# Fused threshold attention and bilinear ffn: v made stationary, x produced transposed, ffn per batch, and TensorE held to the written order

## The chip, the cores and the metric

The kernel runs on one core of a Trainium2 chip. The metric is device time in microseconds (us). Executions of one kernel on one chip agree within about 1%; times are medians of several runs. All runs compared below are of the fast state unless it is said otherwise.

The engines are TensorE (PE; its weight loads are listed as PEld), VectorE (DVE), ScalarE (ACT), GpSimd (POOL) and the DMA queues that SyncE (SP) starts. They run side by side and wait for one another by semaphores.

## The reference, cut to what matters

```python
# q, k, v: (8 batches, 8 heads, 576 positions, 64), float32
scores = q @ k.transpose(0, 1, 3, 2) / 8
thresh = max(scores, axis=-1) - tau
scores = where(scores >= thresh, scores, -1e9)
attn   = softmax(scores)                        # (denominator + 1e-9)
x      = (attn @ v) as (4608 tokens, 512)       # heads side by side
out    = ((x @ w_a) * (x @ w_b)) @ w_out        # 512 -> 1536 -> 512
```

The three weight matrices arrive as float64. The kernel turns their bits into float32 on the chip, in 36 pieces of 128 x 512. All products are of float32.

## The kernel before

Two heads of a batch are a pair. A pair is five units of query rows: four main units (128 rows of each head) and a tail unit (the last 64 rows of both heads). There are 32 pairs and 160 units. A unit goes through `scores`, `weigh` (exponent, mask, row sums), `turn` (transposes of the weights on TensorE) and `weighted` (weights times v). The ffn of two batches is spread between the units of the next two. In `weighted` the weights are stationary and v is streamed:

```python
def weighted(i, u):                       # before, cut
    pv = ps_1.tile([P, 2, D], ...)
    for j in range(2):                    # head
        for c in range(NCB + 1):          # block of keys
            ...                           # lhsT (stationary): 128 keys x 128 queries; rhs: 64 columns of v
            nc.tensor.matmul(dst, lhsT, rhs, start=(c == 0), stop=(c == NCB))
    ...                                   # then scaled by 1/sum, and transposed by finish()
```

One piece of weights is converted with five VectorE operations, one of ScalarE and three of GpSimd. The first one of GpSimd is a clamp:

```python
nc.gpsimd.tensor_scalar(top, top, float_of(0x47F00000), float_of(0x38000000),
                        op0=ALU.min, op1=ALU.max)
...
nc.gpsimd.tensor_tensor(low, low, t, op=ALU.mult)
nc.gpsimd.tensor_tensor(low, low, top, op=ALU.add)
```

## Time and profile before

| | before |
|---|---|
| time, median of 3 first runs | 2063.77 us |
| TensorE busy | 97% of the span |
| first ffn matmul | 363 us, after 40 units of attention alone |
| VectorE / ScalarE / GpSimd busy | 36% / 28% / 14% |

Two more views: the first is the chain that ended last, the path of work and waits followed back from the end, as shares of the span by engine:

```profile
PE 89%; POOL 3%; DVE 3%; ACT 2%; issue 1%; SPq 1%; DMA 0%; POOLq 0%; DVEq 0%; ACTq 0%
```

The second is the list of groups of GpSimd. The columns are line, engine, operation, tiles, shapes and count, then busy us and mean ns of one, then the idle time before them and what ended it:

```profile
L150 POOL TENSOR_TENSOR low<-low,top 128x512 f32<-128x512 f32 x36 | 46.3, 1287 | 2.3
L149 POOL TENSOR_TENSOR low<-low,t 128x512 f32<-128x512 f32 x36 | 46.0, 1277 | 39.3 <-DVE t L148 20.4 <-ACT wT L270 15.1 <-ACT low L140 3.4
L142 POOL TENSOR_SCALAR top<-top 128x512 f32<-128x512 f32 x36 | 22.1, 613 | 36.4 <-DVE sums L251 35.6 <-DVE top L141 0.8
```

### The profile page before, as it was taken

The page shows a single profiled execution, that of the slowest core. Times are in us where ns is not written, and L with a number is a line of the kernel's source. Part 1 is how long each engine was busy: PE and PEld are TensorE (multiplying, and loading weights), DVE is VectorE, ACT ScalarE, POOL GpSimd, SP SyncE. Part 2 cuts the span into 40 slices and gives each one's busy share as a digit, 9 for nine tenths or more (in the row PEclk, how much of TensorE's full clock was granted, in tenths as well). Part 3 has the DMA queues.
Part 4 walks back from the last instruction along what each step waited for, and adds up shares of the span by engine and source line. Part 5 has one row for each costly group of instructions (what it writes and reads, how often), then busy time and mean ns, then how long its engine had stood idle before and what let it go on. Part 6 is the DMA issues. An engine that isn't in the chain of part 4 may idle for free.

```text
span 2066.4 us, 24299 instructions
## 1 busy us (share of the span) xinstructions
PE 2002.3 (97%) x9472; PEld 1308.9 (63%) x9472; DVE 753.0 (36%) x1866; ACT 571.1 (28%) x1017; POOL 297.0 (14%) x728
## 2 busy tenths in 40 slices
PE   7788888999999999999999999999999999999999
PEld 5577776665665666665665666666666666655554
DVE  6776765333332333333332332333333333200000
ACT  3444433222222232322222332332222322200000
POOL 4555552000000000000000000000000000000000
PEclk9767767999999999999999999999999999999999
DMA  4322321000001001001000000000100000000000
GB/s 124 86 79 72 90 76 28 18 18 22 17 18 28 17 18 33 18 7 28 23 18 22 23 18 17 23 19 23 28 12 23 16 1 6 11 6 10 11 5 16
DMA packets 125826, 58.20 MB, mean 28 GB/s; under 512 B 116496, under 2 KB 116496, under 8 KB 125712
## 3 DMA queue, kind: packets, MB, share of 16 engines
q1 hardware_dynamic: 120528, 47.21, 9.1%
q10 hardware_dynamic: 5184, 9.44, 1.2%
q8 instruction: 75, 1.23, 0.2%
q14 instruction: 39, 0.32, 0.0%
HBM read 47.19 MB, written 9.44 MB: 27 GB/s over the span
## 4 chain that ended last, share of the span: by engine, by line
PE 89%; POOL 3%; DVE 3%; ACT 2%; issue 1%; SPq 1%; DMA 0%; POOLq 0%; DVEq 0%; ACTq 0%
PE pab L328 36%; PE po L344 18%; PE pv L287 15%; PE sc L222 9%; PE tp L265 6%; PE sc L225 2%; PE tp L269 1%; ACT w L244 1%; POOL low L150 1%; POOL low L149 1%; DVE mx L232 1%; POOL bias L233 1%; ACT wT L266 1%; PE tp L309 1%; DVE w L247 1%
## 5 line engine op out<-in xcount | busy, mean ns | idle before, releaser
L328 PE MATMUL pab<-xT,wa_sb 128*128 128x384 f32 x1152 | 409.3, 490 | 2.2 <-ACT wT L266 2.0
L328 PE MATMUL pab<-xT,wb_sb 128*128 128x384 f32 x1152 | 408.9, 489 | 0.0
L344 PE MATMUL po<-wo_sb,h 128*128 128x512 f32 x864 | 389.7, 596 | 0.1
L232 DVE TENSOR_REDUCE mx<-sc 128x1 f32<-128x576 f32 x288 | 208.1, 753 | 414.4 <-PE sc L222 350.1
L287 PEld LDWEIGHTS pv<-vm,wT 128*128 128x128 f32 (+1 forms) x2560 | 310.3, 193 | 61.8 <-issue 25.4
L287 PE MATMUL pv<-vm,wT 128*128 128x64 f32 (+1 forms) x2560 | 323.2, 276 | 9.9 <-ACT wT L266 9.2
L266 ACT COPY wT<-tp 128x512 f32<-128x512 f32 x288 | 159.1, 589 | 553.2 <-PE tp L265 552.9
L328 PEld LDWEIGHTS pab<-xT,wa_sb 128*128 128x128 f32 x1152 | 211.9, 190 | 133.3 <-ACT wT L266 4.4
L328 PEld LDWEIGHTS pab<-xT,wb_sb 128*128 128x128 f32 x1152 | 212.4, 190 | 130.2
L233 POOL TENSOR_SCALAR bias<-mx,e_nscale 128x1 f32<-128x1 f32 x288 | 99.3, 345 | 1331.0 <-DVE mx L232 1294.7
L244 ACT ACTIVATE w<-sc,bias,e_scale 128x576 f32<-128x576 f32 x288 | 233.2, 845 | 194.3 <-POOL bias L233 188.6
L247 DVE SCALAR_TENSOR_TENSOR w<-sc,thr,w 128x576 f32<-128x576 f32 x288 | 227.8, 815 | 138.9 <-ACT w L244 137.0
L344 PEld LDWEIGHTS po<-wo_sb,h 128*128 128x128 f32 x864 | 157.7, 191 | 163.9 <-issue 159.6
L222 PE MATMUL sc<-kT,qT 64*128 64x64 f32 (+1 forms) x1024 | 222.3, 486 | 37.3 <-DVE w L247 37.0
L222 PEld LDWEIGHTS sc<-kT,qT 64*128 64x128 f32 x1024 | 113.6, 203 | 169.1 <-issue 148.1
L338 DVE TENSOR_TENSOR h<-a,pab 128x384 f32<-128x384 f32 x144 | 79.7, 553 | 353.7 <-PE pab L328 353.7
L335 ACT COPY a<-pab 128x384 f32<-128x384 f32 x144 | 69.6, 484 | 473.0 <-PE pab L328 471.0
L265 PE MATMUL tp<-ident,w 128*128 128x128 f32 x1152 | 181.9, 304 | 0.8 <-DVE qT L202 0.7
L265 PEld LDWEIGHTS tp<-ident,w 128*128 128x128 f32 x1152 | 144.7, 157 | 18.7 <-DVE qT L202 5.0
L291 DVE TENSOR_TENSOR x<-pv,rcp 128x128 f32<-128x128 f32 x128 | 37.1, 290 | 243.2 <-PE pv L287 243.1
L287 PE MATMUL pv<-vt,wT 128*128 128x64 f32 (+1 forms) x640 | 123.4, 276 | 0.0
L287 PEld LDWEIGHTS pv<-vt,wT 128*128 128x128 f32 (+1 forms) x640 | 96.7, 193 | 8.1 <-ACT low L140 3.8
(57 smaller groups left out, 958.1 us busy)
## 6 DMA issues: line engine op xcount, KB each, us to landing
out_dram<-osb ACTq DMA_DIRECT2D x36, 256.0 KB, 2.0
qm<-in_q_dram SPq DMA_DIRECT2D x64, 128.0 KB, 2.9
km<-in_k_dram SPq DMA_DIRECT2D x64, 128.0 KB, 3.0
vm<-in_v_dram SPq DMA_DIRECT2D x64, 128.0 KB, 2.7
raw<-in_moe_w_a_dram SPq DMA_DIRECT2D x12, 512.0 KB, 3.5
raw<-in_moe_w_b_dram SPq DMA_DIRECT2D x12, 512.0 KB, 3.6
raw<-in_moe_w_out_dram SPq DMA_DIRECT2D x12, 512.0 KB, 3.5
qt<-in_q_dram SPq DMA_DIRECT2D x32, 32.0 KB, 2.4
```

The source lines that it names most:

```text
L222: nc.tensor.matmul(sc[j][:, c0:c1], qT[r, u * P:(u + 1) * P], kT[r, c0:c1], start=True, stop=True)
L232: nc.vector.tensor_reduce(mx[:, c], sc[j], axis=AX.X, op=ALU.max)
L233: nc.gpsimd.tensor_scalar(bias[:, c], mx[:, c], e_nscale[:, 0:1], None, op0=ALU.mult)
L244: nc.scalar.activation(w, s, AF.Exp, bias=bias[:, j:j + 1], scale=e_scale[:, 0:1])
L247: nc.vector.scalar_tensor_tensor(out=ws[j], in0=s, scalar=thr[:, j:j + 1], in1=ws[j], op0=ALU.is_ge, op1=ALU.mult, accum_out=sums[:, j:j + 1])
L265: nc.tensor.transpose(tp[:, c, :], w[:, c * P:(c + 1) * P], ident)
L266: nc.scalar.copy(wT[:, j, 0:NCB, :], tp)
L287: nc.tensor.matmul(dst, lhsT, rhs, start=(c == 0), stop=(c == NCB))
L328: nc.tensor.matmul(p, w[:, c, fs], xT[:, c, t0:t0 + NTB], start=(c == 0), stop=(c == HP - 1))
L335: nc.scalar.copy(a, p)
L338: nc.vector.tensor_tensor(h, a, pab[1], op=ALU.mult)
L344: nc.tensor.matmul(po, hs[F][:, u * P:(u + 1) * P], wo_sb[:, F, :], start=(F == 0), stop=(F == NF - 1))
```

## The change

The intent has four parts. v becomes the stationary operand, with 64 columns, so the two heads use the two column halves of TensorE's array of multipliers and x comes out transposed without further transposes. The ffn runs per batch in groups of 512 tokens, with all tails as a ninth group, so it can start after one batch. The weights are therefore divided by their row sums before they are transposed, on GpSimd. And TensorE keeps the order in which the instructions are written, while the other engines are still reordered by a scheduler. The conversion of a weight piece also loses one VectorE operation, and the two bounds of its clamp change places.

```diff
-        nc.gpsimd.tensor_scalar(top, top, float_of(0x47F00000), float_of(0x38000000),
-                                op0=ALU.min, op1=ALU.max)
+        nc.gpsimd.tensor_scalar(mag, mag, float_of(0x38000000), float_of(0x47F00000),
+                                op0=ALU.max, op1=ALU.min)
 ... (rest of the conversion cut: one VectorE operation less)
     def weigh(i, u):
 ...
         nc.vector.reciprocal(rcp[:, 0:n], sums[:, 0:n])
+        for j in range(n):
+            nc.gpsimd.tensor_scalar(ws[j], ws[j], rcp[:, j:j + 1], None, op0=ALU.mult)
 ...
     def weighted(i, u):
-        for j in range(2):
-            for c in range(NCB + 1):
-                rhs = vm[:, c, j, :] if c < NCB else vt[:, j, :]
+        for c in range(NCB + 1):
+            for j in range(2):
                 if u < NCB:
-                    dst, lhsT = pv[:, j, :], wT[:, j, c, :]
+                    rhs = wT[:, j, c, :] if c < NCB else wTt[:, 0, :]
 ...
-                nc.tensor.matmul(dst, lhsT, rhs, start=(c == 0), stop=(c == NCB))
+                nc.tensor.matmul(pv[j * D:(j + 1) * D, 0:cols],
+                                 vm[:, j, c, :] if c < NCB else vt[:, j, :],
+                                 rhs, start=(c == 0), stop=(c == NCB))
 ... (finish(), which transposed x, is gone; ffn(g) takes 512 tokens in place of 3 x 384)
+    ctx.enter_context(tc.manual_schedule(engines={mybir.EngineType.PE}))
-    per_group = GB * HP * (NCB + 1)
+    per_group = HP * (NCB + 1)
 ...
-        convert_weights()
-        load_weights(1)
+        for _ in range(n % 2 if n < per_group else 2):
+            convert_weights()
+            load_weights(1)
```

## The prediction

> **What bounds the kernel now.** I read the page top down: busy shares, slices, groups, then the timeline of one steady unit. Rows of the page:
>
> ```profile
> span 2066.4 us, 24299 instructions
> PE 2002.3 (97%) x9472; PEld 1308.9 (63%) x9472; DVE 753.0 (36%) x1866; ACT 571.1 (28%) x1017; POOL 297.0 (14%) x728
> ...
> PE   7788888999999999999999999999999999999999
> ...
> DVE  6776765333332333333332332333333333200000
> ...
> PEclk9767767999999999999999999999999999999999
> ```
>
> TensorE is the bound, in two stages. In the first seven slices (about 358 us) it runs at three quarters of its clock and not full, while VectorE has its highest load. These are the 40 units of query rows of the first two batches: attention alone, beside the conversion of the weights. After that TensorE is full at full clock. The table of stretches says it with numbers (columns: us, then busy us and instruction counts of PE, PEld, DVE, ACT, POOL, then clock, DMA share, GB/s):
>
> ```profile
> 12.00:358.00 346.00, 299.76 (x1550) 237.09 (x1550) 237.50 (x562) 139.92 (x234) 173.19 (x261) 0.75 0.29 79
> ...
> 400.00:1800.00 1400.00, 1393.90 (x6946) 899.96 (x6945) 477.03 (x1217) 394.25 (x715) 117.40 (x437) 1.00 0.07 19
> 1800.00:2064.00 264.00, 262.75 (x744) 141.13 (x742) 18.71 (x34) 21.04 (x42) 0.00 (x0) 1.00 0.02 8
> ```
>
> Busy time of matmuls overlaps, so I price them by the distance from the start of one row to the start of the next in the timeline of TensorE (start us, us, engine, line, operation, tiles, shapes, count):
>
> ```profile
> 1846.05 24.20 PE L344 MATMUL po<-wo_sb,h 128*128 128x512 f32 x56
> ...
> 1012.41 1.30 PE L222 MATMUL sc<-kT,qT 64*128 64x512 f32 x8
> 1013.64 0.66 PE L265 MATMUL tp<-ident,w 128*128 128x128 f32 x4
> 1014.13 0.27 PE L269 MATMUL tp<-ident,w 128*128 128x128 f32 x1
> 1014.24 0.49 PE L328 MATMUL pab<-xT,wb_sb 128*128 128x384 f32 x1
> ...
> 1042.07 1.00 PE L287 MATMUL pv<-vm,wT 128*128 128x64 f32 x8
> 1042.90 0.39 PE L287 MATMUL pv<-vt,wT 128*128 128x64 f32 x2
> 1043.13 1.06 PE L287 MATMUL pv<-vm,wT 128*128 128x64 f32 x8
> 1044.02 0.39 PE L287 MATMUL pv<-vt,wT 128*128 128x64 f32 x2
> 1044.24 1.51 PE L328 MATMUL pab<-xT,wa_sb 128*128 128x384 f32 x4
> ```
>
> Each fp32 matmul is two records ("passes"), a transpose is one. A 512-column pass costs (24.20 - 0.59)/55 = 0.429 us, the 384-column pass 0.3225 us (8 passes in 2.58 us in the last stage): the same per column. A score pair of two heads is 1.23 us, a transpose 0.12 us (five in 0.60), and the 20 passes of the weighted sum 1042.07 to 1044.24 = 2.17 us, 0.1085 each. That last pass streams 64 columns, which by the rate above would take 0.054 us: it is held up by the load of its 128-column weights.
>
> **What the Trainium skill says.** (1) "TensorE: Matmul & The Clock Gate", LDWEIGHTS: load time is the column count over 1.2, so 107 ns for 128 columns and 53 ns for 64, whatever the rows. The trace agrees: 0.1085 us with 128 columns, and 0.057 us in the tails, which load 64 (1.13 us for 20). (2) "TensorEngine Tiling (Array Packing)", When to Use Tiling, names this change: for a streamed dimension of 64, swap stationary and streaming and tile the columns, up to 2x. It also says under Key Properties that a change of mode drains the array. That two column halves overlap with fp32 here is shown by the tail units, where the second head follows the first in the other 64 columns:
>
> ```profile
> 1018.72 0.22 PE L287 MATMUL pv<-vt,wT 128*64 128x64 f32 x1
> 1018.77 0.22 PE L287 MATMUL pv<-vm,wT 128*64 128x64 f32 x1
> 1018.78 0.22 PE L287 MATMUL pv<-vt,wT 128*64 128x64 f32 x1
> 1018.83 0.46 PE L287 MATMUL pv<-vm,wT 128*64 128x64 f32 x5
> ```
>
> In program order both vt passes of head 0 come before the vm passes of head 1; here they alternate, two starting 10 ns apart, so the halves run side by side. Row halves do so too: a score pair holds four 512-column passes (4 x 0.429 = 1.72 us) and takes 1.23. (3) "SBUF — State Buffer", Who interferes with whom: VectorE and GpSimd exclude each other on a shared port. The trace shows it: one bitwise step of the conversion took 0.42 us alone and 1.35 us beside GpSimd's 1.27 us product. This matters for stage one.
>
> **The change part by part.**
>
> *ffn.* Before: 4 groups x 3 x 96 x 2 = 2304 passes of 384 and 864 of 512: 743 + 371 = 1114 us. After: nine groups (eight batches and one of all tails), 1728 + 864 passes of 512: 2592 x 0.429 = 1113 us. Nothing gained.
>
> *Attention on TensorE, per pair of heads.* Before: a main unit is 1.23 + 10 x 0.12 + 2.17 = 4.60 us; the tail unit 1.02 (scores) + 5 x 0.12 + 1.13 + 0.65 (four transposes of x and the fold) = 3.40; the preparation of q and k 1.28. A pair is 4 x 4.60 + 3.40 + 1.28 = 23.1 us.
> After: v is stationary with 64 columns, so loads (53 ns) hide under 128 streamed columns (107 ns), and the two heads alternate in the two column halves: ten matmuls x 2 passes at two abreast = 10 x 0.1085 = 1.09, with 0.1 for the drain 1.19 us. A main unit has nine transposes (both last 64-column blocks share one): 1.23 + 1.08 + 1.19 = 3.50. The tail: scores in two halves 1.02 again, six transposes 0.72, sum about 0.65, no transpose of x: 2.39. Preparation: nine transposes, 1.08. A pair is 17.5 us, 5.6 less.
>
> *Stage one.* It shrinks from 40 units to 20, as the ffn now starts after one batch. But the instruction order built from the changed kernel puts 31 of the 36 weight conversions into these 20 units (VectorE, ScalarE and GpSimd are still reordered; only TensorE is pinned). VectorE then has 31 x (0.730 + 0.629 + 0.680 + 0.417 = 2.46) = 76 us, one step of 0.69 less per piece than before, and attention: per main unit 2 x (0.753 + 0.815 + 0.083) + 0.33 = 3.63, per tail 1.95, preparation 1.56, so 18.0 per pair, 72 for four. Together 148 us. Before, VectorE was 69% busy there (237.5 of 346). TensorE's work falls from 185 us to 70 and no longer competes, and the exponent no longer waits for GpSimd's bias (188.6 us of ScalarE's waits before), so I choose 80%: 185 us, plus 12 until the first loads land, about 200 us. Before it was 358.
>
> *Stage two.* The scheme must reproduce the kernel before: 24 pairs x 23.1 + 1114 = 1668 us against 2066 - 358 = 1708 measured, so 40 us for 120 units, 0.33 us each, for drains and short waits. After: 28 pairs x 17.5 = 490, ffn 1113, 140 x 0.33 = 46.
>
> *The written order.* TensorE now waits where the text says. Units last about 10 us. The weights of a unit are masked about 6 us after its scores start, then scaled on GpSimd (two at about 0.69 us, scaled from the 0.613 us of a 512-column one): about 8 us, and the transposes come at 11. Score buffers come free at about 6 us and are wanted at 10. Those fit. One does not: in every fourth unit the preparation takes three of the four PSUM buffers just ahead of the transposes. VectorE copies q only after two reductions (2 x 0.753 + 0.682 = 2.2 us after the scores), TensorE wants that buffer 1.1 + 0.5 = 1.6 us after: with the semaphores some 0.8 us x 28 = 22 us.
>
> *Off the path.* Scaling of x on VectorE (37.1 + 18.1 us) goes, pv copies come to ScalarE, 288 scalings (some 200 us) to GpSimd at 14%. None becomes a bound in stage two: VectorE has about 4.5 us per 10 us unit.
>
> Sum: 200 + 490 + 1113 + 46 + 22 + 4 for the last output = **1875 us**, 9% less.
>
> **The rivals.**
> *The column halves run one after the other.* Then a weighted sum stays at 2.17 us (107 ns of streaming takes the place of 107 ns of loading), and the tail scores double: 112 x 0.98 + 28 x 1.36 = 148 us back, 2020 us. The alternation in the tail rows speaks against it.
> *The pinned order starves TensorE.* Before, the reordering left 0.5% idle after 400 us. If each of 140 units lost 1 us more, 2015 us. Against it: the slack of 2 to 4 us above.
> *Stage one becomes a conversion bound.* Twice as many pieces per unit, excluding each other on the shared port: at 60% VectorE it would take 260 us, 1935 in all; at 95% 170 and 1845.
>
> **Range and chances.** Stage one gives +50/-30 us, stalls +40/-30, the halves a one-sided +148 at some 6%. So 1820 to 1935 for 8 in 10. Faster by over 2%: 0.93; within 2%: 0.05 (halves serial, or starvation); slower: 0.02.
>
> **What would show it.** In the profile after: three or four slices of reduced clock in place of seven, the first ffn matmul near 200 us; from a pv row to the next row 1.2 us in place of 2.17, the two heads' records starting in pairs; 2592 ffn passes at 0.429; a wait of the transposes for the copy of q, about 28 times; PE near full from 220 us on. The number is wrong if the pv passes stand 0.107 us apart singly, if waits of TensorE for ScalarE or GpSimd add up to over 60 us in stage two, or if the ffn begins after 260 us.

## The result, and the profile after

The changed kernel takes 1974.33 us (median of 4 runs, 1973.8 to 1974.51) against 2065.66 us for the kernel before in the same session. The ratio is 0.956, 95% interval 0.9526 to 0.9594. A ratio here is the mean time of one kernel's fast runs over that of the other's of the same rounds, so it is not quite the ratio of the medians quoted. The direction was right and the size was not: 1875 us had been forecast, with 1935 as the upper end.

The page of the kernel after, its busy shares and some of its slices:

```profile
span 1972.5 us, 22785 instructions
...
PE 1801.7 (91%) x8704; PEld 951.7 (48%) x8704; DVE 703.9 (36%) x1598; ACT 554.2 (28%) x1141; POOL 722.6 (37%) x600
...
PE   4556569999999999999999999999999999999999
...
POOL 6888894233323333333323333333323332300000
PEclk9666679999999999999999999999999999999999
```

TensorE has less to do than before and idles more: its low stretch still fills six slices of 49 us, although it now covers 20 units instead of 40. What stands at 8 and 9 in those slices is GpSimd, whose busy time rose from 297 to 723 us.

The table of stretches (us, then busy us and counts of PE, PEld, DVE, ACT, POOL, then clock, DMA share, GB/s) puts the boundary at the first ffn matmul, which the timeline has at 259.8 us:

```profile
10.00:260.00 250.00, 140.55 (x773) 100.33 (x774) 149.66 (x295) 80.33 (x154) 211.93 (x149) 0.70 0.30 88
...
308.00:1600.00 1292.00, 1258.92 (x6586) 661.25 (x6585) 467.79 (x1130) 405.35 (x854) 427.84 (x376) 1.00 0.09 23
```

In stage one GpSimd is busy 212 of 250 us (85%), VectorE 150 (60%), TensorE 141 at 0.70 of its clock. In stage two TensorE is busy 97%. The chain of the kernel after, to be read against that of before:

```profile
PE 80%; POOL 9%; DVE 7%; issue 3%; ACT 1%; SPq 0%; DMA 0%; POOLq 0%; DVEq 0%
```

GpSimd went from 3% to 9% of the chain. Its two groups:

```profile
L258 POOL TENSOR_SCALAR w<-w,rcp 128x576 f32<-128x576 f32 x288 | 500.8, 1749 | 355.2 <-DVE rcp L256 333.1 <-PE pab L317 20.8 <-DVE mag L152 1.3
L146 POOL TENSOR_SCALAR mag<-mag 128x512 f32<-128x512 f32 x36 | 73.1, 2030 | 24.6 <-DVE mag L145 16.2 <-DVE rcp L256 6.4 <-DVE sums L255 2.0
```

A scaling takes 1.749 us, where 0.69 had been reckoned. The clamp, with the same two bounds on a tile of the same size, went from 0.613 to 2.030 us. TensorE's own waits, from the list of who waited for whom (us in total, times, longest):

```profile
PE tp L271 <- POOL w L258: 85.1, 47, 7.1
...
PE tp L271 <- DVE qT L199: 30.2, 27, 1.1
```

The transposes of the weights waited 85 us for GpSimd's scalings. The second wait is the one that the prediction named for the written order. The weighted sum did what was expected of it (timeline of TensorE, a main unit: start us, us, engine, line, operation, tiles, shapes, count):

```profile
1512.36 1.09 PE L294 MATMUL pv<-wT,vm 128*64 128x128 f32 x16
1513.29 0.39 PE L294 MATMUL pv<-wTt,v_tail 128*64 128x128 f32 x4
1513.60 1.30 PE L223 MATMUL sc<-kT,qT 64*128 64x512 f32 x8
```

From 1512.36 to 1513.60 is 1.24 us for twenty passes, in place of 2.17.

**Where the 97 us went.** The device time missed 1875 us by 99, the profile's span (1972.5 us) by 97; the table adds up to the span. From the starts of consecutive ffn groups in the timeline of TensorE, one can compare each part with the prediction's terms. The prediction's stage two comes to 203.4 us per batch that has both attention and ffn: (490 + 46 + 22)/7 = 79.7 us for its 20 units and 1113/9 = 123.7 us for its ffn.

| part of the kernel after | predicted us | measured us | difference |
|---|---|---|---|
| start to first ffn matmul (20 units) | 200 | 260 | +60 |
| first batch with ffn | 203.4 | 225.5 | +22 |
| six further batches | 1220.3 | 5 x 206.3 + 203.5 = 1235.0 | +15 |
| two last ffn groups and the output | 251 | 252 | +1 |

### The profile page after: what moved, and what is told of

Same layout as the page of the kernel before. It is cut to its first block, busy times and chain, and to the rows that moved or that the text cites. A ratio compares the mean times of both kernels' runs of the same rounds, so it can differ in the third digit from the quotient of the medians.

```text
span 1972.5 us, 22785 instructions
## 1 busy us (share of the span) xinstructions
PE 1801.7 (91%) x8704; PEld 951.7 (48%) x8704; DVE 703.9 (36%) x1598; ACT 554.2 (28%) x1141; POOL 722.6 (37%) x600
## 4 chain that ended last, share of the span: by engine, by line
PE 80%; POOL 9%; DVE 7%; issue 3%; ACT 1%; SPq 0%; DMA 0%; POOLq 0%; DVEq 0%
PE pab L317 37%; PE po L333 19%; PE pv L294 8%; PE tp L271 7%; PE sc L223 6%; POOL w L258 4%; POOL mag L146 2%; DVE top L235 2%; PE sc L230 2%; DVE w L252 1%; POOL low L153 1%; DVE mag L148 1%; DVE qT L199 1%; PE tp L276 1%; POOL wb_sb L154 0%
## 5 line engine op out<-in xcount | busy, mean ns | idle before, releaser
L258 POOL TENSOR_SCALAR w<-w,rcp 128x576 f32<-128x576 f32 x288 | 500.8, 1749 | 355.2 <-DVE rcp L256 333.1
L235 DVE TENSOR_REDUCE top<-sc 128x1 f32<-128x576 f32 x288 | 206.1, 752 | 498.1 <-PE sc L223 359.9
L317 PE MATMUL pab<-x_main,wb_sb 128*128 128x512 f32 x768 | 363.9, 605 | 4.4 <-ACT a L324 4.4
L317 PE MATMUL pab<-x_main,wa_sb 128*128 128x512 f32 x768 | 359.2, 599 | 0.0
L250 ACT ACTIVATE w<-sc,top 128x576 f32<-128x576 f32 x288 | 206.6, 756 | 147.7 <-DVE top L235 142.0
L317 PEld LDWEIGHTS pab<-x_main,wb_sb 128*128 128x128 f32 x768 | 140.3, 191 | 159.3 <-issue 147.1
L294 PEld LDWEIGHTS pv<-wT,vm 128*64 128x64 f32 x2560 | 143.9, 146 | 133.7 <-issue 68.2
L317 PEld LDWEIGHTS pab<-x_main,wa_sb 128*128 128x128 f32 x768 | 138.7, 191 | 141.5 <-issue 139.9
L294 PE MATMUL pv<-wT,vm 128*64 128x128 f32 (+1 forms) x2560 | 185.5, 285 | 20.9 <-ACT wT L272 20.9
L223 PE MATMUL sc<-kT,qT 64*128 64x512 f32 (+1 forms) x1024 | 182.7, 458 | 19.9 <-DVE w L252 15.7
```

What stands on the lines that cost most here:

```text
L223: nc.tensor.matmul(sc[j][:, c0:c1], qT[r, u * P:(u + 1) * P], kT[r, c0:c1], start=True, stop=True)
L235: nc.vector.tensor_reduce(top[:, j:j + 1], sc[j], axis=AX.X, op=ALU.min)
L250: nc.scalar.activation(ws[j], s, AF.Exp, bias=top[:, j:j + 1], scale=-1.0)
L258: nc.gpsimd.tensor_scalar(ws[j], ws[j], rcp[:, j:j + 1], None, op0=ALU.mult)
L294: nc.tensor.matmul(pv[j * D:(j + 1) * D, 0:cols], vm[:, j, c, :] if c < NCB else vt[:, j, :], rhs, start=(c == 0), stop=(c == NCB))
L317: nc.tensor.matmul(p, w[:, c, fs], xT[:, c, :], start=(c == 0), stop=(c == HP - 1))
```

## The experiments

Theory G: stage one is bound by GpSimd, because two of its operations cost 2.5 and 3.3 times what was reckoned. Rival C: stage one is a chain of latencies, stretched by TensorE's halved clock and by the pinned order, beside which GpSimd only looks busy. A further rival, about the gain, is that the column halves do not overlap. The experiments change one thing each, but for e3 and for f1 to f3, which keep the old clamp order besides. The columns "first ffn", "first batch" and "steady batch" are read from the timeline as above. The first two have to be read together: the scheduler put 31 of the 36 clamps before the first ffn matmul in the kernel after and in e2, but 25 in e1 and e3, 27 in e6, 10 in e7 and 34 in f1, and the rest fell into the first batch.

| run | first ffn | first batch | steady batch | time (median) | ratio to before |
|---|---|---|---|---|---|
| kernel after | 260 | 225.5 | 206.3 | 1974.3 | 0.956 |
| e1_scale_dve | 193 | 239.6 | 205.4 | 1915.4 | 0.928 |
| e2_clamp_order | 224 | 220.1 | 206.3 | 1933.0 | 0.936 |
| e3_both | 176 | 227.0 | 205.4 | 1885.9 | 0.913 |
| e4_unpinned | 232 | 245.9 | 203.2 | 1950.4 | 0.945 |
| e5_heads_in_turn | 259 | 237.1 | 218.8 | 2060.4 | 0.997 |
| e6_clamp_twice | 278 | 256.7 | 206.3 | 2023.6 | 0.979 |
| e7_pin_all | 207 | 318.2 | 206.3 | 2013.2 | 0.974 |
| f1_scale_act | 197 | 206.7 | 205.6 | 1888.4 | 0.914 |
| f2_act_unpinned | 173 | 217.7 | 202.7 | 1858.4 | 0.900 |
| f3_act_prep_later | 179 | 211.8 | 201.9 | 1854.1 | 0.898 |
| f4_scale_constant (one run, wrong result) | 218 | 248.9 | 205.7 | 1952.1 | - |

e5 and e7 are medians of two runs, the others but f4 of four. The e runs were made in two sessions and the f runs in a third. Across sessions the ratios compare better than the times: the medians of the kernel before were 2068.9, 2068.5 and 2067.9 us.

### e1_scale_dve: the scaling on VectorE

```diff
-            nc.gpsimd.tensor_scalar(ws[j], ws[j], rcp[:, j:j + 1], None, op0=ALU.mult)
+            nc.vector.tensor_scalar(ws[j], ws[j], rcp[:, j:j + 1], None, op0=ALU.mult)
```

> Theory G: stage one (up to 308 us in the profile after) is bound by GpSimd, whose scalings take 1.75 us and clamps 2.03 us where I had reckoned 0.69 and 0.61. Moving the scalings to VectorE takes some 42 x 1.8 = 75 us from GpSimd in stage one and puts some 17 us on VectorE: stage one ends near 230 us and the total is about 1895 us (1880 to 1920). Rival C (the halved clock and the written order make stage one a chain of latencies, GpSimd only looks busy): a gain of at most 20 us, 1955 or more. Stage two stays at 1664 us under both, as GpSimd had slack there.

Measured: 1915.4 us, 59 less than the kernel after, where rival C allowed 20. The group of the scaling now reads:

```profile
L258 DVE TENSOR_SCALAR w<-w,rcp 128x576 f32<-128x576 f32 x288 | 157.4, 584 | 5.1
```

VectorE does in 0.584 us what GpSimd did in 1.749 (0.99 on average in stage one, beside the conversions, and 0.53 later). The first ffn matmul comes 67 us earlier. The first batch, which holds the 11 conversions that are left over (5 in the kernel after), takes 14 us longer. A steady batch changes by only 0.9 us, so in stage two the slow scaling was hidden, as predicted.

### e2_clamp_order: the two bounds in the old order

```diff
-        nc.gpsimd.tensor_scalar(mag, mag, float_of(0x38000000), float_of(0x47F00000),
-                                op0=ALU.max, op1=ALU.min)
+        nc.gpsimd.tensor_scalar(mag, mag, float_of(0x47F00000), float_of(0x38000000),
+                                op0=ALU.min, op1=ALU.max)
```

> The clamp with its two bounds in the order of the kernel before (smaller of, then larger of), same values. If the order of the two operations sets the duration, one clamp takes about 0.61 us again, and theory G says 36 x 1.3 = 47 us less in stage one: about 1927 us (1915 to 1940). If contention with VectorE made the clamps slow, they stay near 2 us and the time at 1974. Rival C: clamps get short but the time stays over 1960.

Measured: 1933.0 us, 41 less, for an edit that changes no value. The row of the clamp:

```profile
L146 POOL TENSOR_SCALAR mag<-mag 128x512 f32<-128x512 f32 x36 | 25.6, 712 | 24.6 <-DVE mag L145 16.2 <-DVE rcp L256 6.4 <-DVE sums L255 2.0
```

The mean falls from 2.030 to 0.712 us, so the order of the operations sets the duration and contention with VectorE adds little. In each of the two traces 11 clamps had no VectorE instruction beside them: they took 0.605 to 0.609 us here and 1.917 to 1.923 in the kernel after.

### e3_both: the two together

The edits of e1 and e2.

> Both at once. Theory G: GpSimd falls to about 125 us of work in stage one and VectorE (about 165 us) is next; stage one ends near 200 us and the total is about 1866 us (1850 to 1890), which is where the prediction stood. If the two gains do not add, another bound came first: about 1890.

Measured: 1885.9 us, 88 less than the kernel after. That is 20 above what was expected here (1866), inside the range, but nearer the 1890 given for gains that do not add: the two gains alone were 59 + 41 = 100. It is 11 above the prediction's 1875. Stage one of this kernel in the table of stretches:

```profile
10.00:176.00 166.00, 118.31 (x772) 85.56 (x772) 152.57 (x307) 73.25 (x146) 96.04 (x95) 0.81 0.39 111
```

GpSimd is down to 96 of 166 us, and VectorE, which now has the scalings too, is at 153, 92%. Stage one is shorter than predicted (176 us against 200) but it holds 25 clamps instead of 31, and the first batch, with the rest of them, is as much longer (227.0 against 203.4). Together they take 403.1 us, where the prediction had 403.4 and the kernel after took 485.3. That VectorE is the bound now is not shown: f1 below speaks against it.

### e4_unpinned: without the written order

```diff
-    ctx.enter_context(tc.manual_schedule(engines={mybir.EngineType.PE}))
```

> The changed kernel without the pinned order of TensorE. Theory G: GpSimd does the same work in stage one, so the time is within 1% of 1974 (1955 to 1990). Rival C: the written order is what starves TensorE, so stage one shortens by 40 us or more and the time falls to 1935 or less. Stage two loses at most the 22 us reckoned for the preparation.

Measured: 1950.4 us, 24 less, just outside G's range and well short of C's 1935. The ffn starts 28 us earlier and its first batch takes 20 us longer, so what the reordering takes forward is mostly given back. A steady batch takes 203.2 us in place of 206.3, and the wait for the copy of q shrinks from 30.2 us:

```profile
PE tp L271 <- DVE qT L199: 3.4, 13, 0.3
```

That is the prediction's term for the written order: as an estimate, 3.1 us x 7 batches = 22 us; the six batches after the first gave 17 (5 x 3.1 + 1.7).

### e5_heads_in_turn: the halves not alternated

```diff
-        for c in range(NCB + 1):
-            for j in range(2):
+        for j in range(2):
+            for c in range(NCB + 1):
```

> The ten matmuls of a weighted sum in head order (five of head 0, then five of head 1) instead of alternating, nothing else. If the two column halves run side by side only when neighbours in the stream are of different halves, a weighted sum takes about 2.1 us in place of 1.25 and the time grows by some 112 x 0.9 + 28 x 0.45 = 113 us in stage two, to about 2087 us (2050 to 2110). If TensorE finds the other half anyway, the time stays within 1% of 1974.

Measured: 2060.4 us, 0.997 of the kernel before, interval 0.9921 to 1.0017. A weighted sum (timeline of TensorE):

```profile
1092.26 1.15 PE L294 MATMUL pv<-wT,vm 128*64 128x128 f32 x10
1093.18 0.27 PE L294 MATMUL pv<-wTt,v_tail 128*64 128x128 f32 x1
1093.24 0.27 PE L294 MATMUL pv<-wT,vm 128*64 128x128 f32 x1
1093.29 0.27 PE L294 MATMUL pv<-wTt,v_tail 128*64 128x128 f32 x1
...
1094.20 2.84 PE L333 MATMUL po<-wo_sb,h 128*128 128x512 f32 x6
```

It takes 1.94 us in place of 1.24. The passes of head 0's last block (wTt) mix with the first ones of head 1 (wT), so some overlap happens at the seam, which is why the loss is 86 us and not the 113 expected. Without the alternation the whole change, as it was built, is worth nothing: the alternation of the two halves was worth 86 us, and all else in it, the slow GpSimd operations included, came to about zero.

### e6_clamp_twice: the suspected cost doubled

```diff
         nc.gpsimd.tensor_scalar(mag, mag, float_of(0x38000000), float_of(0x47F00000),
                                 op0=ALU.max, op1=ALU.min)
+        nc.gpsimd.tensor_scalar(mag, mag, float_of(0x38000000), float_of(0x47F00000),
+                                op0=ALU.max, op1=ALU.min)
```

> The clamp twice in a row (the second changes no value): 36 x 1.93 = 69 us more of GpSimd, all in stage one. Theory G (GpSimd bounds stage one): 55 to 70 us more, 2030 to 2045 us. Rival C (a latency chain through TensorE, with GpSimd beside it): under 25 us more, below 2000.

Measured: 2023.6 us, 49 more. That is 0.7 of the 69 us added, below G's 55 to 70 and twice C's limit of 25. Only 18 us of it lie before the first ffn matmul and 31 in the first batch, as 4 conversions more were left for that batch. GpSimd is the main bound while weights are converted, but not a pure one: about a third of the added work fell into time in which it had waited anyway (it was 85% busy in stage one).

### e7_pin_all: the written order on the other engines too

```diff
-    ctx.enter_context(tc.manual_schedule(engines={mybir.EngineType.PE}))
+    ctx.enter_context(tc.manual_schedule(engines={mybir.EngineType.PE, mybir.EngineType.DVE,
+                                                  mybir.EngineType.Activation, mybir.EngineType.Pool}))
```

> VectorE, ScalarE and GpSimd keep the written order as well, so only 10 of the 36 conversions lie in stage one and 26 beside the ffn. Theory G: GpSimd has 10 x 4.6 + 40 x 1.75 + 6 = 122 us in stage one, which ends near 170 us; the 13 units with two conversions then need 2 x 4.6 + 3.8 = 13 us of GpSimd against 10 of TensorE, 40 us back: about 1880 us (1850 to 1930). Where the strict order makes engines wait for each other in every unit, it is slower than 1974.

Measured: 2013.2 us, outside the range; the other branch of the expectation, slower than 1974, held. Stage one did shorten, to 207 us and not to 170, but the first batch with ffn grew to 318 us. Its row of stage one in the table of stretches:

```profile
10.00:207.00 197.00, 133.19 (x772) 91.79 (x770) 83.47 (x207) 62.61 (x129) 109.97 (x88) 0.73 0.21 56
```

Neither GpSimd (110 of 197 us, 56%) nor VectorE (83, 42%) is full, so neither one's work alone sets the pace here, which fits rival C's chain of latencies. In written order VectorE stands still while GpSimd clamps (VectorE's second conversion step):

```profile
L148 DVE TENSOR_SCALAR mag<-mag 128x512 uint32<-128x512 uint32 x36 | 15.4, 427 | 170.5 <-POOL mag L146 170.5
```

The 170.5 us of idle time before 36 steps are 4.7 us each; in the kernel after, the scheduler had filled most of it with other work (53.6 us in all). Spreading the conversions is no remedy as long as each makes the engines wait for each other.

### e8_before_pinned: the pin alone, on the kernel before

```diff
+    ctx.enter_context(tc.manual_schedule(engines={mybir.EngineType.PE}))
     units = [(i, u) for i in range(NPR) for u in range(NCB + 1)]
```

> The kernel before with TensorE's instructions kept in the written order and nothing else. If the pin is neutral by itself: within 1% of 2066. If the scheduler's reordering was worth what it looked like (TensorE 0.5% idle after 400 us), the pin costs 1 us or more per unit there: 2100 to 2250 us.

Measured: 2069.1 us, ratio 1.0011, interval 0.998 to 1.0042: the same. The pin by itself neither gains nor loses in the old kernel.

### f1_scale_act: the scaling on ScalarE, with the old clamp order

```diff
-            nc.gpsimd.tensor_scalar(ws[j], ws[j], rcp[:, j:j + 1], None, op0=ALU.mult)
+            nc.scalar.mul(ws[j], ws[j], rcp[:, j:j + 1])
```

> Clamp order as in the kernel before, and the scalings on ScalarE in place of GpSimd (in the run with both changes VectorE did them and stood at 173 us busy of 188 in stage one, ScalarE at 80). Some 42 x 0.59 = 25 us leave VectorE in stage one and reach ScalarE at about 0.75 us each. If VectorE is the bound that followed GpSimd: 1861 to 1875 us. If a chain of latencies is the bound by now, ScalarE's longer operation in it makes it no faster than the run with both changes: 1880 or more.

Measured: 1888.4 us, ratio 0.9142 against 0.9132 of e3: no faster. A scaling takes 0.77 us on ScalarE:

```profile
L258 ACT ACTIVATE w<-w,rcp 128x576 f32<-128x576 f32 x288 | 209.5, 770 | 175.3 <-DVE rcp L256 175.2
```

The first ffn matmul comes later than in e3 (197 against 176 us) and the first batch is shorter by as much (206.7 against 227.0), as 34 clamps and not 25 came before it; together they take 403.5 us, against 403.1. So relieving VectorE did not help; my expectation of 1861 to 1875 was wrong, and its other branch held. What bounds this stage now, VectorE or the sequence of small waits, these runs do not separate.

### f2_act_unpinned and f3_act_prep_later: two ways around the wait for q

f2 is f1 without the pin. f3 is f1 with the pin and the preparation of the next pair after the transposes:

```diff
-        if u == 3 and i + 1 < NPR:
-            prep(i + 1)
         if before is not None:
             turn(*before)
         weigh(i, u)
+        if u == 3 and i + 1 < NPR:
+            prep(i + 1)
```

> The same without the pinned order of TensorE. In the unpinned kernel a steady batch took 203.2 us in place of 206.3 but the first ffn batch 245.9 in place of 225.5. With conversions cheaper for GpSimd, I expect 7 x 3 = 21 us less in stage two and no large loss in the first batch: 1840 to 1865 us. If the first batch loses 20 us again, it equals the pinned one.

> The same with the pin, and the preparation of the next pair written after the transposes of the unit in place of before. If the wait of the transposes for the copy of q (28 waits of about 0.8 to 1.1 us) is what the pin costs, a steady batch falls from about 205.5 to 202.5 us and the total by 20 us: 1842 to 1858. If the wait only moves to the preparation, nothing changes.

Measured: f2 1858.4 us, f3 1854.1 us, both inside their ranges. In f3 a steady batch takes 201.9 us in place of 205.6. So in the steady batches the pin's cost was the one wait, and it can be written away. Of the 34 us between f1 and f3 the batches after the first explain 21 (5 x 3.7 + 2.8); the other 13 lie before them, f2 gains them too, and their cause is not shown. f3 is the fastest version, by 4 us over f2, 0.898 of the kernel before (interval 0.8939 to 0.9012) and 120 us under the kernel after.

### f4_scale_constant: what makes the scaling slow

```diff
-            nc.gpsimd.tensor_scalar(ws[j], ws[j], rcp[:, j:j + 1], None, op0=ALU.mult)
+            nc.gpsimd.tensor_scalar(ws[j], ws[j], 0.5, None, op0=ALU.mult)
```

> Wrong result on purpose: GpSimd scales by the constant 0.5 in place of a value per row, all else as in the changed kernel. If the operand per row makes the scaling slow, one takes about 0.69 us in place of 1.73 and the time falls to about 1900 to 1925 us. If a single multiplication is slow on GpSimd whatever its operand, it stays at 1.73 us and 1974.

The result is wrong on purpose. One run of unknown state, 1952.1 us. The row of the scaling:

```profile
L258 POOL TENSOR_SCALAR w<-w 128x576 f32<-128x576 f32 x288 | 476.9, 1671 | 210.5 <-DVE w L252 208.7
```

1.671 us against 1.749: the operand per row costs 0.08 us. Nor is it contention: in the kernel after, 210 of the 288 scalings had no VectorE instruction beside them and took 1.718 to 1.739 us. A single multiplication of 576 elements per row is slow on GpSimd in these traces, and the 22 us less may come from no longer waiting for the reciprocal; one run does not settle that.

## Why the prediction was wrong

*The step that failed* is in "The written order" and "Off the path": GpSimd's scaling was reckoned as "two at about 0.69 us, scaled from the 0.613 us of a 512-column one", "some 200" us in all, and the clamp, 0.613 us in the profile before, was not priced anew: the part on stage one adds up VectorE's work and leaves GpSimd's out. The 0.613 us was the price of one particular pair of operations, smaller-of followed by larger-of. A multiplication costs 1.7 us for 576 columns, and the swapped pair 1.9 to 2.0 us for 512. The measured sum for scalings is 500.8 us. In stage one 36 scalings and 31 clamps took 129 us of GpSimd, where the reckoned durations give 44 (36 x 0.69 + 31 x 0.613). The Trainium skill's page "GPSIMD Engine Reference", Engine selection, says that one-input operations run roughly at line rate on GpSimd; this trace differs (1.749 us on GpSimd, 0.584 on VectorE for the same operation), and the measurement decides.

*The consequence* fell where there was no slack. In stage one the prediction took VectorE at 80% as the bound and 200 us as its length. VectorE's work was about as reckoned (150 us against 148), but it was only 60% busy: GpSimd at 85% was the main bound, and the stage lasted 260 us, with another 22 us lost in the first batch with ffn, where the left-over conversions ran. Correcting the two operations (e3) gives 1886 us: 88 of the 99 us missed are shown to be theirs, with the caveat that e3 also loads VectorE. The third rival, "stage one becomes a conversion bound", had the right place and, at 60% VectorE, the right length of 260 us, but the wrong engine: it blamed the exclusion of VectorE and GpSimd. VectorE's steps are stretched beside GpSimd, but e2 gained its 41 us almost without changing that: the four steps of a piece took 3.08 us on average in the kernel after, 3.02 in e2, and 1.96 in e7, where three of the four never overlapped with GpSimd. Of the three signs that were to tell that the number is wrong, none quite fired: the sum's passes did not stand singly, the ffn began at 259.8 us where 260 was the limit, and after that TensorE waited only 19 us for GpSimd and ScalarE together, where 60 was the limit.

*The ffn at 1113 us* was right: the last two groups took 123.7 and 123.6 us, and 1113/9 = 123.7.

*The weighted sum at 1.19 us* was right in kind and 0.05 us short. The rival of halves in turn is refuted: e5 shows 1.94 us without the alternation.

*The written order at 22 us* named the right wait and was a little low: 27 waits of 1.1 us, 30.2 in total, where 28 of 0.8 had been reckoned; unpinning gives back 3.1 us per steady batch, and f3 removes it. The rival that the pin starves TensorE is refuted in the old kernel (e8) and limited to 24 us in the new one (e4).

*The remaining 0.33 us per unit* for drains and waits was a little low: steady batches took 2.9 us more than 203.4, 15 us over six of them. About 1.2 us of the 2.9 are those longer waits ((30.2 - 22)/7), and another 1.2 are parts that took longer than reckoned: scores and sum of the tail unit 1.12 + 0.73 us, where 1.02 + 0.65 stood, and the preparation 1.20, where 1.08 stood, four of each per batch. The rest is not shown.

*Left open:* why GpSimd's durations depend so much on the operation (no run looks inside it), and what bounds stage one after e3, since f1 moved work from VectorE to ScalarE without any gain, and e7 was slow there with no engine full.

## What to carry to other kernels

An engine that is idle on average can be the bound of a stage: price every operation that is moved to it from a row of the same operation, and where there is none, measure it alone before trusting a neighbour's duration. Here two column halves of TensorE overlapped when the matmuls alternated between them (1.24 us per sum against 1.94 in turn), and the loop order alone decided it. A pinned order costs what its waits cost; look for the one wait that repeats and move the instruction that causes it.

## What the Trainium skill lacked or had wrong

- "GPSIMD Engine Reference", Engine selection: one-input operations are called roughly line-rate. Here a multiplication of 128 x 576 f32 by a value per row took 1.749 us on GpSimd, 1.671 with a constant, 0.584 on VectorE and 0.770 on ScalarE.
- No page that I read says that the order of two operations in one GpSimd instruction changes its duration: smaller-of then larger-of took 0.613 us (kernel before) and 0.712 (e2), larger-of then smaller-of 2.030 us, for 128 x 512 f32 and the same bounds.
- "TensorE: Matmul & The Clock Gate", Part 3, says that weight loads overlap matmuls in flight only when the row group differs. Here they overlapped with all 128 rows in use by both, even without column halves: in the ffn of the kernel after, a load of 128 x 128 f32 began with the matmul before it (at 1517.43 us, lasting 0.19 us), and the matmuls still started every 0.429 us.
